# Building the experts' token lists in SBUF by one-hot matmuls, with slots of 128 tokens and another split of the early weights' subtraction

## The chip, the core and the metric

The kernel runs on one core of a Trainium2 chip, as one launch. The metric is the time of that launch on the device in microseconds (us). A core has a matrix engine (TensorE: PE for its matmuls, PEld for its weight loads in the profile), three elementwise engines (VectorE: DVE, ScalarE: ACT, GpSimd: POOL) and a queue engine (SyncE: SP) that here only issues transfers. Each engine works through its own instructions in order; semaphores hold one until another engine or a transfer is done.

## What is computed

A gated linear attention over 4 batches, 8 heads, 768 positions and head size 48, whose output rows (384 wide) go through a mixture of 8 experts with sticky routing:

```python
for t in range(S):                                   # attention
    state = alpha[:, :, t, :, None] * state + einsum('bhd,bhe->bhde', k[:, :, t], v[:, :, t])
    y[:, :, t] = einsum('bhd,bhde->bhe', q[:, :, t], state)
...
fresh_e = argmax(logits[b, s])                       # routing, token after token
e = fresh_e if s == 0 or local_gate[b, s] < 0.5 else prev_e
p = exp(ls) / (exp(ls).sum() + 1e-09)                # ls: logits less their largest
out[b, s] = p[e] * (relu(x[b, s] @ w1[e]) @ w2[e])   # w1: 384x1024, w2: 1024x384
```

So there are 3072 tokens, each for one expert, and which expert is known only after routing.

## The kernel before

**Attention.** 24 blocks of 128 tokens (`NB`), one after the other, four batches in turn (`G` = 4). The loop at L637 runs stages of several blocks in one turn: scans of alpha on DVE (`scan1`, `scan2`: tiles `A`, `sf`), their products with q and k on POOL (tile `x`), transposes and small matmuls on PE (`kt`, `pm`, `um`, `ym`, `xt`: PSUM tiles `kp`, `pe`, `up`, `y`, `xp`), masks and sums on DVE (`pq`, `st`), copies on ACT (`kk`, `sb`, `XR`, `vt`, `xx`). Each block's rows are stored to the DRAM tensor `xd`. From L629 to L695 instructions are pinned: every engine keeps the order in which the code was written.

**Side work.** `other()` (L589) is called three times a turn. It flushes deferred work (`later`), advances each running `route` by one piece (up to its next `yield`) and then either issues two filler matmuls (`dense`, on tile `dz`) or one piece of the early expert work.

**Routing.** `route(g)` (L417) handles a group of four blocks: logits (`lg`), transposes (`lt`, `rp`, `rb`), the sticky choice by a scan (`em`), one-hot of the expert (`oh`), softmax weight (`se`, `pn`, `pl`), prefix sums over tokens (`oi`, `pw`, `ps`, `po`) and, as `ix`, the row of each token in its expert's list. A list row holds the weight, the token's number and its row in `xd`. The lists live in the DRAM tensor `ls`, which is first filled with an empty entry (`fill`, L623 to L626); `route` scatters 128 entries for each block by an indirect DMA on POOL (L512).

**Experts.** A `Job` covers some rows of one expert's list in slots of 120 tokens: `load_list` reads rows of `ls` into `li` (SP), `gather` fetches the tokens' rows of `xd` (indirect DMA on POOL, tile `xg`), `trans` transposes them on PE (`tp`) and splits them into a high part (`xh`, ACT) and the rest (`xl`, DVE); `gemm1` makes `h` (72 matmuls, three for each product of split operands), split likewise into `hh` (ACT) and `hl` (DVE); `gemm2` makes `yp` (24 matmuls of 384 columns for a slot); `store` scales it by the weight (`yo`, DVE) and scatters it into `out` (indirect DMA on POOL). `Weights` loads an expert in seven pieces into staging tiles (`rw`, four buffers, on SP), takes the high part on ACT (`w1h`, `w2h`) and subtracts for the rest (`w1l`, `w2l`) on POOL or DVE.

**Early jobs.** `early()` (L526) starts once the first 12 blocks (`T1`) are routed. It runs three jobs within the attention's last part: the first 240 rows of expert 0 (job 0), the first 240 of expert 1 (job 1), and the other 240 of expert 1 (job 2), for which all blocks must be routed. Expert 1's subtractions run on POOL, as do those of expert 2 (`NEXT`). During the early jobs all transposes share one PSUM buffer (`tr`), with `kp` and `xp` of the attention. Behind them come experts 2 to 7 with 480 rows each and the other 240 rows of expert 0; there a scheduler sets the order.

**Tail.** A table of overflowing tokens is made (L721 to L732), and a loop that does not run with these data follows (L734).

Of the kernel before, what the change touches and what calls it, by code (L numbers as in the profile page):

```python
# [29 lines left out]
NS = CAP // SL  # L30
NOV = -(-(NTOK - CAP) // SL)
RS = CAP + NOV * SL
SENT = NTOK
ZTHR = -1.5 * 2.0 ** -23
# [5 lines left out]
C1 = 240  # L40
# [8 lines left out]
RW = 4  # L49
# [15 lines left out]
def gla_moe(ctx, tc, akq, vw, vn, wg, w1, w2, cst, tok, out):  # L65
# [28 lines left out]
    fill = cp.tile([SL, E * NS, 3], F32, name="fill")  # L94
# [15 lines left out]
    outs, lists, rest = [], [], []  # L110
# [47 lines left out]
    class Job:  # L158


        def __init__(self, e, r0, n, sp, ps, bx, bg, bh, by, pb, rows=NTOK + 1, bt=2, defer=lambda f: f()):
            self.e, self.r0, self.n, self.sp, self.ps = e, r0, n, sp, ps
            self.ns = n // SL
# [55 lines left out]
        def gemm2(self, W):  # L219
            for s in range(self.ns):  # L220
                w = slice(s * SL, (s + 1) * SL)
                yp = self.ps.tile([SL, DM], F32, tag=self.yt[s % len(self.yt)], bufs=self.pb[2], name=f"yp_{self.nm}_{s}")
# [8 lines left out]
                yo = self.sp.tile([SL, DM], F32, tag="yo", bufs=self.by, name=f"yo_{self.nm}_{s}")  # L231
# [10 lines left out]
    with ExitStack() as ac, ExitStack() as aa:  # L242
# [6 lines left out]
        dz = ap.tile([128, 512], F32R, bufs=1, name="dz")  # L249
# [3 lines left out]
        v_.tensor_copy(dz, z2[:, 0:512])  # L253
# [14 lines left out]
        st = {"c": c0}  # L268
        blk = {}
# [84 lines left out]
        def um(i):  # L354
# [3 lines left out]
            if i < G:  # L358
                s3 = ap.tile([R, 3, HP, D], F32, tag="st", bufs=G + 2, name=f"st_{i}")
# [57 lines left out]
        def route(g):  # L417
# [4 lines left out]
            def rt(shape, nm, dt=F32):  # L422
                return ap.tile(shape, dt, tag=nm, name=f"{nm}_{g}")
# [5 lines left out]
            lc = rt([128, 128], "lc")  # L429
# [14 lines left out]
            mb = mx.unsqueeze(2).broadcast_to([128, n, 8])  # L444
            ge = rt([128, n, 8], "ge")
            v_.tensor_tensor(ge, L8, mb, ALU.is_ge)
            v_.tensor_tensor(ge, ge, cc("desc").unsqueeze(1).broadcast_to([128, n, 8]), ALU.mult)
            m2 = rt([128, n], "m2")
            v_.tensor_reduce(m2, ge, AX.X, ALU.max)
            v_.tensor_tensor(ge, ge, m2.unsqueeze(2).broadcast_to([128, n, 8]), ALU.is_equal)  # L450
            zb = L[:, :, 8:9].broadcast_to([128, n, 8])
            v_.scalar_tensor_tensor(kr[:, 0], zb, ZTHR, ge, ALU.is_lt, ALU.mult)
            v_.tensor_single_scalar(kr[:, 1], zb, ZTHR, ALU.is_ge)
# [6 lines left out]
            km = rt([8 * n, 128], "km")  # L460
            s_.copy(km, rp[:, 1, :])
# [50 lines left out]
            for j in range(n):  # L512
# [3 lines left out]
                if j < n - 1:  # L516
                    yield
# [119 lines left out]
        for i in range(NB + 2):  # L637
# [4 lines left out]
            if i < NB:  # L642
                kt(i)
# [236 lines left out]
```

## Time and profile before

| | us |
|---|---|
| median of 3 runs | 498.49 (497.36 to 499.62) |
| the profiled execution | 495.6 |
| its span, first to last instruction | 493.8 |
| mean granted TensorE clock | 0.945 of full speed |

| engine | busy us | share of the span |
|---|---|---|
| PE | 434.4 | 88% |
| PEld | 391.0 | 79% |
| DVE | 250.2 | 51% |
| POOL | 232.2 | 47% |
| ACT | 181.1 | 37% |

A row of the profile's views reads: start and duration (or, for a group, busy time and mean ns), engine, source line, operation, the tile written `<-` the tiles read, sizes, count, and in brackets the idle time of the engine just before it with what ended that idle time. Most rows have one line, L79, since a wrapper records the operations: the tiles' names tell them apart.

### The profile page before, as it was taken

The numbers are of one execution on the slowest core, as the hardware profiler recorded it, in microseconds if no ns is written. First come the engines' busy times: TensorE is split into PE (matmuls) and PEld (weight loads), VectorE is DVE, ScalarE is ACT, GpSimd is POOL, SyncE is SP. The second block draws the span as 40 slices with busy tenths as digits, with TensorE's granted clock in tenths as the row PEclk, the third lists the DMA queues.
The fourth block names the chain that finished last, engine by engine and source line by source line (L and its number), as shares of the span: only waits on it lengthen the run. The fifth ranks groups of instructions, "written<-read, shape, count | busy, mean of one in ns | idle before, by whom it ended". The sixth has DMA issues, their size and how long they took to land.

```text
span 493.8 us, 10848 instructions
## 1 busy us (share of the span) xinstructions
PE 434.4 (88%) x4395; PEld 391.0 (79%) x4395; DVE 250.2 (51%) x440; ACT 181.1 (37%) x350; POOL 232.2 (47%) x245
## 2 busy tenths in 40 slices
PE   4999878989897888487979999999999999999990
PEld 4787767768775778486958998998998999989990
DVE  3878997989796526622222434334253253333320
ACT  1255654545443624221443423423334234233210
POOL 6453336464747335847385254353624735424201
PEclk9799998999988899798887999999999999999995
DMA  8789775797573011454155256254254452540100
GB/s 222 176 284 269 218 197 104 222 244 199 158 182 94 33 48 33 120 132 120 53 156 154 65 173 182 73 171 126 85 156 124 156 177 58 171 144 1 50 2 27
DMA packets 30058, 66.14 MB, mean 134 GB/s; under 512 B 7694, under 2 KB 13979, under 8 KB 30007
## 3 DMA queue, kind: packets, MB, share of 16 engines
q1 hardware_dynamic: 20022, 49.70, 36.7%
q0 software_dynamic: 4864, 10.66, 7.4%
q10 hardware_dynamic: 5121, 5.07, 3.1%
q8 instruction: 35, 0.57, 0.5%
q14 instruction: 16, 0.13, 0.1%
HBM read 55.89 MB, written 10.70 MB: 135 GB/s over the span
## 4 chain that ended last, share of the span: by engine, by line
PE 52%; issue 10%; DVE 7%; POOL 2%; ACT 2%; DMA 1%; POOLq 0%; ACTq 0%; DVEq 0%
PE h L79 23%; PE yp L79 21%; PE y L79 3%; PE tp L79 2%; DMA ls<-pl,ix 1%; PE up L79 1%; POOL out L79 1%; DVE sf L79 1%; DVE A L79 1%; PE pe L79 1%; PE lg L79 1%; DVE hl L79 1%; POOL w1l_0b L79 1%; DVE xl L79 1%; DVE oi L79 1%
## 5 line engine op out<-in xcount | busy, mean ns | idle before, releaser
L79 DVE SCALAR_TENSOR_TENSOR hl<-h,hh 128x480 fp32r<-128x480 f32 (+1 forms) x80 | 44.2, 555 | 91.5 <-ACT hh L79 82.7
L79 ACT ACTIVATE hh<-h 128x480 fp32r<-128x480 f32 (+1 forms) x80 | 39.0, 490 | 89.8 <-PE h L79 79.9
L79 POOL DMA_INDIRECT xg<-xd,li x32 | 34.8, 1088 | 48.9 <-DMA li<-ls 25.2
L79 POOL DMA_INDIRECT out<-yo,li x32 | 32.5, 1016 | 47.7 <-DVE yo L79 42.9
L79 DVE TENSOR_SCALAR yo<-yp,li 120x384 f32<-120x384 f32 x32 | 19.6, 617 | 63.9 <-PE yp L79 61.6
L79 POOL TENSOR_TENSOR x<-x,sf 112x512 f32<-112x512 f32 x24 | 28.9, 1205 | 32.8 <-DVE sf L79 32.8
L79 POOL TENSOR_TENSOR x<-x,A 112x512 f32<-112x512 f32 x24 | 29.3, 1221 | 29.2 <-DVE A L79 8.7
L79 DVE TENSOR_TENSOR_SCAN A<-a,z 112x520 f32<-112x520 f32 x24 | 32.5, 1352 | 6.8 <-POOL a L79 6.8
L79 PE MATMUL h<-dz 128*128 128x240 f32 x142 | 33.0, 337 | 2.3 <-DVE z L79 2.3
L79 POOL DMA_INDIRECT ls<-pl,ix x24 | 25.5, 1061 | 18.6 <-DVE hl L79 7.8
L79 DVE TENSOR_TENSOR_SCAN sf<-a,z 112x520 f32<-112x520 f32 x24 | 33.8, 1407 | 0.1
L79 PE MATMUL y<-vt,pq 64*64 64x48 f32 x768 | 30.0, 224 | 3.3 <-issue 3.3
L79 PEld LDWEIGHTS y<-vt,pq 64*64 64x64 f32 x768 | 26.1, 138 | 8.2 <-issue 8.0
L79 ACT COPY sb<-st 48x384 f32<-48x384 f32 x48 | 24.5, 510 | 15.3 <-DVE st L79 14.7
L79 PE MATMUL y<-sb,x 112*64 112x96 f32 x384 | 23.8, 270 | 6.2 <-ACT sb L79 6.1
L79 PEld LDWEIGHTS h<-dz 128*128 128x128 f32 x142 | 22.5, 213 | 6.9 <-DVE z L79 2.3
L79 PE MATMUL tp<-cs,xg 120*128 120x120 f32 x96 | 14.8, 282 | 12.3 <-DVE xl L79 12.3
L79 PEld LDWEIGHTS y<-sb,x 112*64 112x64 f32 x384 | 18.7, 149 | 8.5 <-ACT sb L79 7.2
L79 PE MATMUL up<-vt,kk 128*48 128x96 f32 (+1 forms) x384 | 23.3, 269 | 0.0
L79 PEld LDWEIGHTS tp<-cs,xg 120*128 120x128 f32 x96 | 11.5, 146 | 14.9 <-DVE xl L79 13.8
L79 DVE TENSOR_TENSOR xl<-tp,xh 128x360 fp32r<-128x360 f32 x32 | 16.0, 526 | 11.6 <-ACT xh L79 10.2
L79 ACT COPY XR<-y 128x384 f32<-128x384 f32 x24 | 11.5, 480 | 27.7 <-PE y L79 22.0
(229 smaller groups left out, 1235.0 us busy)
## 6 DMA issues: line engine op xcount, KB each, us to landing
x<-akq SPq DMA_DIRECT2D x24, 448.0 KB
a<-akq SPq DMA_DIRECT2D x24, 227.9 KB
vt<-vn SPq DMA_DIRECT2D x24, 192.0 KB
xd<-XR ACTq DMA_DIRECT2D x24, 192.0 KB
rw_0a<-w SPq DMA_DIRECT2D x3, 512.0 KB
rw_0a<-w SPq DMA_DIRECT2D x4, 384.0 KB
rw_1a<-w SPq DMA_DIRECT2D x3, 512.0 KB
rw_1a<-w SPq DMA_DIRECT2D x4, 384.0 KB
```

Source lines behind the costliest of these rows:

```text
L79: r = f(*a, **k)
```

## The change

- **Lists in SBUF.** `route` no longer scatters. From the token's place (`plc`) it works out the list's slot column (`sl`) and the row in the slot (`rr`), builds one-hots of both (`oa`: 32 columns, `on`: 128 rows), multiplies the slot one-hot with the token's three values (`vo`), and four matmuls (`lp`: on transposed times vo, 96 columns) add the entries at their places; `acc` sums them over the groups, and `idx` holds the token numbers and rows as whole numbers. For the first five groups `on` is made on ACT (two activations for a block) and `vo` on POOL, for the last both on DVE. The filling of `ls` and the read of it (`load_list`'s DMA) are gone; `load_list` now only names slices of `idx` and `acc`. The scatter of all lists stands in the overflow branch, which does not run.
- **Slots of 128.** `TS` = 128: a job of 480 rows has slots of 128, 128, 128 and 96; jobs 0 and 1 have 256 rows, job 2 and the last job 224. `dz` and the filler matmuls are 256 wide.
- **Early weights.** Expert 1's and expert 2's subtractions run on DVE, and there are three staging buffers instead of four (`RW`).
- **Order.** `route` is a piece shorter up to `rb`; deferred work is flushed earlier in the turn; `early` starts with fewer empty pieces; transposes of the next job are put between matmuls of `gemm2`, not behind each other; constants are set up in the first blocks (`made`).

```diff
-RW = 4
+RW = 3
+TS = 128
+NS = -(-CAP // TS)
+WH = 1.5 * 2.0 ** 23
-C1 = 240
+C1 = 256
...
-        def load_list(self):
-            self.li = self.sp.tile([SL, self.ns, 3], F32, tag="li", bufs=self.bx, name=f"li_{self.nm}")
-            r = self.e * RS + self.r0
-            y_.dma_start(self.li, ls[r:r + self.n].rearrange("(p s) c -> p s c", p=SL))
+        def load_list(self, v):
+            c = slice(self.r0 // TS, self.r0 // TS + self.ns)
+            self.tok, self.row = (idx[:, v, k, self.e, c] for k in range(2))
+            self.pr = acc[:, 0, self.e, c]
...
+            pl = vals[:, g * n:(g + 1) * n]
-            g_.tensor_copy(pl.bitcast(I32)[:, :, 1], tk[:, 2 * g:2 * NB:2 * NBB])
-            g_.tensor_copy(pl.bitcast(I32)[:, :, 2], tk[:, 2 * g * G + 1:2 * (g + 1) * G:2])
...
-            for j in range(n):
-                apart(lists, g_.indirect_dma_start(
-                    out=ls[:, :], out_offset=bass.IndirectOffsetOnAxis(ap=ix[:, j:j + 1], axis=0),
-                    in_=pl[:, j, :], in_offset=None, bounds_check=E * RS - 1, oob_is_err=False))
+            pt = rt([128, n], "pt")
+            v_.tensor_scalar(pt, pc, 1.0 / TS, None, ALU.mult)
+            sl = rt([128, n], "sl")
+            v_.tensor_scalar(sl, pt, -(TS - 1) / (2.0 * TS), WH, ALU.add, ALU.add)
+            rr = rt([128, n], "rr")
+            v_.scalar_tensor_tensor(rr, sl, WH, pt, ALU.subtract, ALU.subtract)
+            oa = rt([128, n, E * NS], "oa", bufs=1)
+            v_.tensor_tensor(oa, ioa.rearrange("p e s -> p (e s)").unsqueeze(1).broadcast_to([128, n, E * NS]),
+                             sl.unsqueeze(2).broadcast_to([128, n, E * NS]), ALU.is_equal)
+            yield
+            (v_ if end else g_).tensor_tensor(vo, oa.unsqueeze(2).broadcast_to([128, n, 3, E * NS]),
+                                              pl.unsqueeze(3).broadcast_to([128, n, 3, E * NS]), ALU.mult)
+            if end:
+                v_.tensor_tensor(on, iob.unsqueeze(1).broadcast_to([128, n, TS]),
+                                 rr.unsqueeze(2).broadcast_to([128, n, TS]), ALU.is_equal)
+            else:
+                for j in range(n):
+                    s_.activation(on[:, j], iob, AF.Abs, bias=rr[:, j:j + 1], scale=-1.0)
+                    s_.activation(on[:, j], on[:, j], AF.Relu, bias=one[:, 0:1], scale=-float(TS))
+                    if j < n - 1:
+                        yield
+            yield
+            for j in range(n):
+                t_.matmul(lp, lhsT=on[:, j], rhs=vo[:, j].rearrange("p k s -> p (k s)"), start=(j == 0), stop=(j == n - 1))
+            v_.tensor_tensor(af, af, lp, ALU.add)
+            if end or (g + 1) * G == T1:
+                v_.tensor_tensor(idx[:, int(end)], acc[:, 1:3], off, ALU.add)
...
                     if k % 4 < 2 or k == 2:
                         next(ws, None)
+                    if next(ts, True) is None:
+                        yield False
+                    if not nx and k == 1:
+                        ts = rest[0].trans()
...
+                    if nx and k == (6 if nx.r0 else 3):
+                        ts = nx.trans()
...
-                    begin(NEXT, g_)
+                    begin(NEXT, v_)
...
-                begin(EARLY[1], g_)
+                begin(EARLY[1], v_)
```

Where instructions stand now. The first place is DVE between job 0's last `hl` and job 1's first. Before, from the group's choice to the first transposed slot of job 1:

```order
L79 SCALAR_TENSOR_TENSOR em_2989<-km_2973,em_2699,rp_2970 32x128
L79 TENSOR_TENSOR ex_2925<-L_2902,mx_2926 128x32
L79 SCALAR_TENSOR_TENSOR oi_3025<-m_73,oh_105 128x40
L79 TENSOR_REDUCE se_3028<-ex_2925 128x4
L79 TENSOR_SCALAR se_3028<-se_3028 128x4
L79 RECIPROCAL se_3028<-se_3028 128x4
L79 TENSOR_SCALAR yo_0_0_3045<-yp_0_0_2992,li_0_2345 120x384
...
L79 TENSOR_REDUCE ix_3077<-po_3080 128x4
L79 TENSOR_TENSOR xl_0_3087<-tp_0_0_3088,xh_0_3086 128x3x120
L79 TENSOR_TENSOR xl_0_3087<-tp_0_1_3098,xh_0_3086 128x3x120
```

In the changed kernel, on DVE, the same stretch up to that slot:

```order
L81 TENSOR_TENSOR w1l_1a_3035<-rw_1a_1557,w1h_1a_3034 128x1024
L81 TENSOR_TENSOR acc<-acc,lp_3044 128x96
L81 TENSOR_TENSOR w1l_1a_3053<-rw_1a_1559,w1h_1a_3052 128x1024
L81 TENSOR_TENSOR w1l_1a_3071<-rw_1a_1561,w1h_1a_3070 128x1024
L81 TENSOR_SCALAR yo_0_0_3079<-yp_0_0_3013,acc 128x384
L81 SCALAR_TENSOR_TENSOR em_3085<-km_3065,em_2770,rp_3062 32x128
L81 TENSOR_TENSOR w2l_1a_3100<-rw_1a_3050,w2h_1a_3099 128x768
L81 TENSOR_TENSOR xl_0_3103<-tp_0_0_3104,xh_0_3102 128x3x128
L81 SCALAR_TENSOR_TENSOR oi_3111<-m_80,oh_112 128x40
```

The subtractions of expert 1 (`w1l_1a`, `w2l_1a`) now stand on DVE ahead of `em`, and the transposed slot's rest stands ahead of `oi`. Further on DVE, behind the list's last place, the changed kernel has these rows, for which there was none before but the `yo`:

```order
L81 TENSOR_REDUCE plc<-po_3150 128x4
L81 TENSOR_SCALAR pt_3153<-plc 128x4
L81 TENSOR_SCALAR sl_3155<-pt_3153 128x4
L81 SCALAR_TENSOR_TENSOR rr_3157<-sl_3155,pt_3153 128x4
L81 TENSOR_TENSOR oa_3159<-ioa,sl_3155 128x128
L81 TENSOR_SCALAR yo_0_1_3167<-yp_0_1_3087,acc 128x384
L81 TENSOR_TENSOR vo_3172<-oa_3159,vals 128x384
L81 TENSOR_TENSOR on_3174<-iob,rr_3157 128x512
L81 TENSOR_TENSOR w2l_1a_3177<-rw_1a_3097,w2h_1a_3176 128x768
L81 TENSOR_TENSOR acc<-acc,lp_3180 128x96
```

They end in the last group's lists. On PE, job 1's two transposes before, within job 0's second slot:

```order
L79 MATMUL yp_0_1_3055<-w2h_0a_1177,hl_0_3_2894 120x384
L79 MATMUL tp_0_0_3088<-cs,xg_0_0_2904 128x120 x3
L79 MATMUL tp_0_1_3098<-cs,xg_0_1_2936 128x120 x3
L79 MATMUL yp_0_1_3055<-w2h_0a_1315,hh_0_4_2917 120x384
```

and in the changed kernel, on PE, around the same two:

```order
L81 MATMUL rb_3094<-cs,em_3085 128x32
L81 MATMUL tp_0_0_3104<-cs,xg_0_0_2905 128x128 x3
...
L81 MATMUL yp_0_1_3087<-w2l_0a_1202,hh_0_3_2865 128x384
L81 MATMUL yp_0_1_3087<-w2h_0a_1201,hl_0_3_2866 128x384
L81 MATMUL tp_0_1_3132<-cs,xg_0_1_2935 128x128 x3
L81 MATMUL pw_3139<-oi_3111,one 128x40
```

Six matmuls now stand between the two transposes, and `rb` and `pw` of the last group stand next to them.

More of the change, by code (lines that the diff above doesn't have):

```diff
@@ L93, in gla_moe @@
     wgs = cp.tile([128, 3, 32], F32, name="wgs")
[L94 removed]
+    fill = cp.tile([SL, 3], F32, name="fill")
+    vals = cp.tile([128, NB, 3], F32, name="vals")
+    plc = cp.tile([128, NB], F32, name="plc")
+    acc = cp.tile([128, 3, E, NS], F32, name="acc")
+    off = cp.tile([128, 2, E, NS], F32, name="off")
+    idx = cp.tile([128, 2, 2, E, NS], I32, name="idx")
+    ioa = cp.tile([128, E, NS], F32, name="ioa")
+    iob = cp.tile([128, TS], F32, name="iob")
     cntp = cp.tile([8, 1], F32, name="cntp")
@@ L108, in gla_moe @@
     ident = cc("ident")
-    outs, lists, rest = [], [], []
+    outs, rest = [], []
     def apart(those, w):
@@ L162, in __init__ @@
             self.e, self.r0, self.n, self.sp, self.ps = e, r0, n, sp, ps
-            self.ns = n // SL
+            self.ns = -(-n // TS)
+            self.w = [slice(s * TS, min(n, (s + 1) * TS)) for s in range(self.ns)]
+            self.m = [w.stop - w.start for w in self.w]
             self.bx, self.bg, self.bh, self.by, self.pb = bx, bg, bh, by, pb
@@ L268, in gla_moe @@
         st = {"c": c0}
+        sts = [ap.tile([R, 3, HP, D], F32, tag="st", bufs=G + 1, name=f"st_{i}") for i in range(G)]
         blk = {}
@@ L504, in route @@
             v_.tensor_tensor(po, ps[:, :, 0:n].rearrange("p e b -> p b e"), ob, ALU.mult)
-            with nc.allow_low_precision(reason="whole numbers, one of them not zero"):
-                v_.tensor_reduce(ix, po, AX.X, ALU.add)
+            pc = plc[:, g * n:(g + 1) * n]
+            v_.tensor_reduce(pc, po, AX.X, ALU.add)
             st["c"] = ps[:, :, n]
@@ L521, in begin @@
         def begin(e, sub):
-            EW[e] = Weights(e, f"{e}a", 4, later.append, sub)
-            for _ in range(4):
+            EW[e] = Weights(e, f"{e}a", RW, later.append, sub)
+            for _ in range(RW):
                 EW[e].load()
@@ L550, in early @@
                     yield True
+                    if not nx and k == 2:
+                        rest[0].load_list(1)
+                    if not nx and k == 5:
+                        for _ in rest[0].gather():
+                            pass
                     if nx and nx.r0 == 0 and k == 2:
@@ L650, in gla_moe @@
                 drained[0] = True
+            for _ in range(min(3, len(made))):
+                made.pop(0)()
             other(i >= NB)
@@ L757, in gla_moe @@
         v_.tensor_copy(ei[:, NOV:], tab[0:1, 0, :])
+        px = mp.tile([128, NB], I32, bufs=1, name="px")
+        v_.tensor_copy(px, plc)
+        pv = mp.tile([128, NB, 3], F32, bufs=1, name="pv")
+        v_.tensor_copy(pv[:, :, 0], vals[:, :, 0])
+        v_.tensor_scalar(pv.bitcast(I32)[:, :, 1], vals[:, :, 1], float(SENT), None, ALU.add)
+        v_.tensor_copy(pv.bitcast(I32)[:, :, 2], vals[:, :, 2])
+        lists = []
+        for i in range(NB):
+            apart(lists, g_.indirect_dma_start(
+                out=ls[:, :], out_offset=bass.IndirectOffsetOnAxis(ap=px[:, i:i + 1], axis=0),
+                in_=pv[:, i, :], in_offset=None, bounds_check=E * RS - 1, oob_is_err=False))
         with tc.For_i(0, NT, 1) as i:
```

129 lines of the change are left out of this document (64 added, 65 removed).

## The prediction

> **What bounds the kernel now.** I read the busy time by stage first, cut where the program's stages begin on PE. The columns are a stretch and its length, then the busy time of each engine with its instructions, PE's granted clock, and the DMA engines' share and rate.
>
> ```profile
> core 0: us, PE busy (x) PEld busy (x) DVE busy (x) ACT busy (x) POOL busy (x), PEclk, DMA share, GB/s
> 19.93:69.18 49.25, 44.70 (x905) 37.46 (x904) 42.55 (x67) 26.85 (x56) 20.81 (x30) 1.00 0.82 238
> 69.18:98.69 29.51, 25.76 (x469) 21.23 (x468) 25.48 (x50) 14.69 (x32) 14.89 (x20) 0.94 0.62 161
> 98.69:124.94 26.25, 23.59 (x469) 19.62 (x468) 24.12 (x45) 12.69 (x30) 14.87 (x18) 1.00 0.84 231
> 124.94:152.01 27.07, 22.35 (x452) 18.54 (x451) 22.86 (x45) 12.18 (x30) 16.41 (x20) 0.94 0.63 162
> 152.01:176.10 24.09, 20.15 (x357) 16.61 (x356) 12.40 (x31) 11.14 (x26) 10.78 (x11) 0.86 0.17 51
> 176.10:207.53 31.43, 22.66 (x165) 21.11 (x166) 16.79 (x33) 11.37 (x24) 17.16 (x14) 0.89 0.23 66
> 207.53:227.31 19.78, 17.33 (x124) 16.82 (x124) 4.53 (x13) 2.98 (x8) 11.74 (x9) 1.00 0.43 110
> 227.31:243.73 16.42, 12.57 (x78) 11.46 (x77) 4.39 (x10) 3.41 (x9) 8.52 (x8) 0.79 0.34 97
> 243.73:260.08 16.35, 11.91 (x62) 10.55 (x61) 3.82 (x8) 8.73 (x13) 11.69 (x6) 0.84 0.47 128
> 260.08:281.13 21.05, 21.05 (x95) 18.40 (x96) 7.91 (x13) 8.11 (x16) 7.10 (x5) 0.88 0.43 120
> 281.13:480.80 199.67, 199.67 (x1104) 188.03 (x1102) 73.83 (x116) 65.72 (x105) 84.40 (x59) 1.00 0.39 114
> ```
>
> From 281.13 to 480.80 PE is never idle at full clock, and its matmuls there are the same in number and in moving columns after the change, so nothing is to be had in those 199.67 us. In the attention (to 152.01) DVE is busy for 84 to 92% and PE for 83 to 91%: both fill. From 152.01 to 260.08 neither does; PE is idle 3.9, 8.8, 2.5, 3.9 and 4.4 us in the five stretches, and its clock falls. The gain has to come from these and from DVE's waits in the attention.
>
> Next, the timeline (start, duration, engine, operation, and the idle time before it with its cause) and the groups of POOL and PE.
>
> ```profile
> L79 POOL DMA_INDIRECT ls<-pl,ix x24 | 25.5, 1061 | 18.6 <-DVE hl L79 7.8
> L79 PE MATMUL tp<-cs,xg 120*128 120x120 f32 x96 | 14.8, 282 | 12.3 <-DVE xl L79 12.3
> 80.27 0.69 DVE L79 TENSOR_TENSOR pq<-pe,cs 128x512 f32<-128x512 f32 x1 [2.61 <-remote]
> 134.34 0.69 DVE L79 TENSOR_TENSOR pq<-pe,cs 128x512 f32<-128x512 f32 x1 [2.68 <-remote]
> 159.89 0.36 DVE L79 TENSOR_TENSOR st<-up,st 112x192 f32<-112x192 f32 x1 [3.85 <-remote]
> 192.36 4.76 POOL L79 TENSOR_TENSOR w1l_1a<-rw_1a,w1h_1a 128x1024 fp32r<-128x1024 f32 x2 [5.71 <-ACT oh L79]
> 192.39 2.48 DVE L79 TENSOR_TENSOR_SCAN oi<-m,oh 128x40 f32<-128x40 f32 x1 [1.31 <-ACT oh L79]
> 200.09 0.19 DVE L79 TENSOR_TENSOR ps<-pw,ps 128x40 f32<-128x40 f32 x1
> 203.54 0.86 PE L79 MATMUL tp<-cs,xg 120*128 120x120 f32 x3 [6.34 <-DVE xl L79]
> ```
>
> The 24 scatters come in six bursts of four, and the "remote" waits stand where a burst is going on: 2.61 and 2.68 us in the first and third, 3.85 in the fourth. Beside a subtraction on POOL (2.38 us each) the small scan `oi` takes 2.48 us, where the small `ps` without one takes 0.19. The last group's choice, prefix sums and `xl` all stand in that row of DVE, and PE waits 6.34 us for the `xl`.
>
> **The change part by part**, against the profiled 495.6 us (2.9 below the median of 498.49).
>
> *Start, -1.0.* The filling of `ls` goes out of POOL's way.
>
> ```profile
> 7.41 0.23 POOL L79 COPY fill<-tk 120x32 int32<-120x32 int32 x1 [1.10 <-DMA tk<-tok]
> ```
>
> POOL waits 1.10 us for `tk` there, with the memset behind it that DVE's first `A` needs. Ends: 0 (the start is bound by a transfer) and -1.3 (wait and copy).
>
> *First eight blocks, +0.4.* Some fourteen constants are set up beside 42.55 of 49.25 us of DVE work, three of them on DVE; with `ps` for each that is 0.6, and 0.2 of it I take as hidden. The ends are 0 and, by `pq` (0.69), 2.1.
>
> *Middle of the attention, -3.7.* In each group the four scatters go, and DVE gets four small operations and `acc` more than it loses: 5 x 0.19 = 1.0 by `ps`, at most 5 x 0.69 = 3.5 by `pq`. I take the smaller, since `pt`, `sl` and `rr` are 128x4. DVE's waits go: 2.61 + 2.68 and, in the second burst, some 1.4 less 0.
>
> ```profile
> DVE pq L79 <- PE pe L79: 1.4, 1, 1.4
> ```
>
> That row (waits of DVE from 98.69 to 124.94: total, times, longest) is all that DVE waits there. So 29.51 becomes 27.9, 26.25 becomes 25.9 and 27.07 becomes 25.4: -3.7 in all. Ends: -6.7 (what is added lies in what is left of DVE's idle time) and +1 (the chain of the blocks keeps its pace, and what is added is paid for). The eight activations that make `on` cost ACT 8 x 0.26 by the row below, in stretches in which it is idle for half the time; POOL gets `vo` (128x384, below the 1.22 us of `x`) for four scatters of 1.06. Either only delays `lp`, and nothing waits for `lp` until a job reads its list.
>
> ```profile
> L79 ACT COPY lc<-lg 128x128 f32<-128x128 f32 x6 | 1.5, 258 | 1.2 <-PE lg L79 1.2
> L79 POOL TENSOR_TENSOR x<-x,A 112x512 f32<-112x512 f32 x24 | 29.3, 1221 | 29.2 <-DVE A L79 8.7
> ```
>
> *Last four blocks, +1.5.* Without the read of `ls` and with fewer empty pieces job 0 starts earlier: 36 of its 72 matmuls for `h` now stand ahead of the last `y`. The chain of work gives their time:
>
> ```profile
> 260.08 8.31 PE h L79 x27
> 329.86 5.90 PE h L79 x27
> ```
>
> 5.90 / 27 x 256/480 x 36 = 4.2 us, and 0.4 for `lp`, against 3.9 us of idle PE. If every gap could be filled the stretch would grow by 0.7; I take 1.5. Ends: 0 and 4.6.
>
> *The seam, 31.43 to 27.0, -4.4.* PE's 22.66 us lose those 4.2: 18.5. Four waits stand in DVE's new order:
>
> ```profile
> L79 DVE TENSOR_TENSOR w1l_0a<-rw_0a,w1h_0a 128x1024 fp32r<-128x1024 f32 x3 | 4.8, 1592 | 2.1 <-ACT w1h_0a L79 2.1
> L79 DVE TENSOR_TENSOR w2l_7b<-rw_7b,w2h_7b 128x768 fp32r<-128x768 f32 x4 | 3.8, 959 | 3.8 <-ACT w2h_7b L79 3.7
> ```
>
> Expert 1's rest now costs DVE 3 x 1.59 + 4 x 0.96 = 8.6 us in the seam, where POOL did it before, and the small operations no longer take 2 us each. Queued behind it: `em`, for which PE's `rb` waits, some 1.6 (one `w1l`); `xl` behind a `w2l`, 1.3 with the copy; `pw` for `oi`, 0.6; `lp` for `on` and the last `w2l`, 3.0 (the 128x512 `on` about as `pq`, two products, and a `w2l`). 18.5 + 6.5 = 25.0, and I add 2.0 for waits too small to be told apart, as DVE has nearly 20 us of work there. Ends: 23 (half of the waits lie under PE's queue) and 31.4 (DVE's row as long as the old one).
>
> *Job 1, -2.3; job 2, -3.0; expert 2's transposes, -2.0; its first matmuls, -1.0.* Transposes now stand between matmuls of `gemm2`, so that `xl` is made beside them. What PE waited for, and its clock in two pieces of these stretches:
>
> ```profile
> 215.61 0.38 PE L79 MATMUL h<-xh,w1h_1a 128*128 128x240 f32 x1 [1.59 <-DVE hl L79]
> 228.79 0.53 PE L79 MATMUL tp<-cs,xg 120*128 120x120 f32 x3 [1.17 <-DVE xl L79]
> 252.94 0.53 PE L79 MATMUL tp<-cs,xg 120*128 120x120 f32 x3 [1.41 <-DVE xl L79]
> 203.50:207.50 4.00, 3.96 (x15) 3.94 (x16) 0.53 (x1) 1.92 (x3) 2.95 (x3) 0.57 0.43 132
> 233.00:237.50 4.50, 4.40 (x20) 4.41 (x21) 0.45 (x2) 0.37 (x1) 3.56 (x4) 0.50 0.48 134
> ```
>
> Job 1 loses its idle 2.45, less what `hl` still costs. Job 2 has 3.9 of idle time and 2.2 lost to a clock of 0.50 for 4.4 us; half goes. Expert 2's 4.4 of idle time would go too, but its 8.6 us of subtraction now stand on DVE with four `xl` and the `yo`, nearly as long as `gemm2`: I take 2.0. Its first `h` group took 8.31 where a later one takes 5.90; 1.0 of the 2.4 goes. Ends together: -15 (all idle time and all slow clock) and -1.
>
> The trace has 4.4 us at half clock from 233.00 on, though no wait ahead of it is above 1.2 us. The Trainium skill (TensorE: Matmul & The Clock Gate, "HAM oscillation — how this bites in real kernels") warns only of idle gaps above about 3.4 us. The 6.34 us gap followed by 0.57 agrees with it, 233.00 does not; I go by the trace.
>
> Sum: -1.0 + 0.4 - 3.7 + 1.5 - 4.4 - 2.3 - 3.0 - 2.0 - 1.0 = -15.5: 480.1 in the profiled execution, and **483.0** beside the median of 498.49.
>
> **The rivals.** *The clock stays full* (470, between 466 and 475). The seam's waits are single and short now, and the 8 us lost to slow clock (1.7, 2.2, 2.4 and what lies between) all go, with the middle's last 3 us. For it: the only long wait, 6.34, goes. Against it: 233.00. By the skill's rule above, this would be the outcome.
>
> *DVE takes the waits' place* (488 to 496, about 492). DVE carries 17.2 us more in the seam and behind it, and 1 us in each group. If each small operation waits for a 1.59 us subtraction, seam, job 2 and expert 2 keep their length: 483.0 + 4.4 + 3.0 + 2.0 = 492.4. For it: the DVE of the middle is 84 to 92% busy. Against it: from 176.10 to 260.08 it is busy for 29.5 of 84 us.
>
> *The scatters were hidden anyway, no change* (496 to 501). Every stretch is bound by the blocks' chain, and the early jobs wait for the weights. The stretch without a burst (19.93 to 69.18) has 6.2 us a block, those with one 7.4, 6.6 and 6.8, which speaks against it.
>
> *Slower: three staging buffers.* A layer's seven pieces come every 199.67 / 6 / 7 = 4.75 us, and a cast waits for its transfer:
>
> ```profile
> 387.55 1.05 ACT L79 CAST w1h_7b<-rw_7b 128x1024 fp32r<-128x1024 f32 x1 [3.71 <-DMA rw_7b<-w]
> 399.48 0.84 ACT L79 CAST w2h_7b<-rw_7b 128x768 fp32r<-128x768 f32 x1 [3.42 <-DMA rw_7b<-w]
> ```
>
> PE does not wait for it now. With one buffer less each load is issued a piece later; if that uncovers one wait of 3.71 us in each of six layers, 22 us are added to PE's unbroken stretch: 483.0 + 22 = 505. It decides from where a transfer comes more than some 3 us (two thirds of a piece's period) later than now. Against it: the DMA share there is 0.39.
>
> **How the numbers follow.** The forecast (475 to 488) has 0.55: most of its terms have a wait in a row that goes. The full clock has 0.17, DVE in the waits' place 0.18, no change 0.04, slower 0.06. About 0.5% (2.5 us) is what a measurement of this kernel can tell from no change, so faster is 0.55 + 0.17 + 0.18 = 0.90, same 0.04, slower 0.06. The range of 469 to 493 takes in the forecast and most of its two neighbours (0.12 and 0.13 of them), and leaves out the tail of both and what is not faster.
>
> **What would show it.** No "remote" wait of DVE from 69 to 160, and blocks 8 to 19 in 79 instead of 82.8 us; half of job 0's `h` ahead of the last `y`; no wait of PE above 3 us in the seam and the seam below 28; `tp` without waits for `xl`; PE without a gap in the six layers. It is wrong if DVE's waits in the middle come back under other names, if `em`, `xl` or `hl` stand behind subtractions for longer than one of them, or if `w1h` of the later experts delays PE.

## The result, and the profile after

The changed kernel took 482.17 us (median of 4 runs, 481.29 to 484.0) beside 497.93 for the kernel before (494.44 to 499.62): a ratio of 0.9735, with an interval from 0.9687 to 0.9782. 483.0 had been forecast, in a range of 469 to 493. The profiled execution was the slowest of the four, 484.0 us with a span of 482.2, 11.6 less than the span before.

The windows view of the changed kernel, cut at the same places of the program as the rows of before (length, then busy time of each engine, PE's clock, DMA):

```profile
core 0: us, PE busy (x) PEld busy (x) DVE busy (x) ACT busy (x) POOL busy (x), PEclk, DMA share, GB/s
...
18.54:69.33 50.79, 46.37 (x906) 38.88 (x905) 42.87 (x72) 27.13 (x56) 22.13 (x35) 0.97 0.75 217
69.33:96.72 27.39, 24.48 (x477) 20.49 (x476) 24.78 (x53) 17.78 (x41) 12.71 (x12) 1.00 0.67 192
96.72:121.81 25.09, 24.36 (x477) 20.51 (x477) 22.96 (x55) 15.47 (x39) 12.72 (x15) 1.00 0.78 235
121.81:144.23 22.42, 21.60 (x459) 17.96 (x459) 21.52 (x40) 14.46 (x36) 12.56 (x13) 1.00 0.67 193
144.23:175.65 31.42, 25.84 (x401) 21.77 (x400) 14.72 (x41) 15.18 (x38) 9.40 (x8) 0.89 0.14 39
175.65:201.30 25.65, 19.29 (x146) 17.17 (x146) 16.24 (x46) 12.82 (x28) 2.92 (x3) 1.00 0.34 100
201.30:223.25 21.95, 20.30 (x123) 19.59 (x123) 5.76 (x15) 3.07 (x8) 11.01 (x11) 0.84 0.50 144
223.25:239.19 15.94, 12.49 (x79) 11.41 (x78) 4.34 (x10) 3.38 (x9) 0.99 (x1) 0.79 0.02 6
239.19:251.24 12.05, 10.47 (x62) 8.87 (x61) 8.98 (x14) 7.43 (x11) 5.20 (x5) 1.00 0.59 186
251.24:269.46 18.22, 18.22 (x91) 16.00 (x92) 7.36 (x11) 7.53 (x14) 7.81 (x6) 1.00 0.63 191
269.46:469.30 199.84, 199.84 (x1104) 186.11 (x1103) 75.84 (x120) 66.56 (x108) 74.84 (x51) 1.00 0.37 110
```

| stage | before, us | forecast change | after, us | change |
|---|---|---|---|---|
| start | 19.93 | -1.0 | 18.54 | -1.4 |
| first eight blocks | 49.25 | +0.4 | 50.79 | +1.5 |
| middle, y8 to y20 | 82.83 | -3.7 | 74.90 | -7.9 |
| last four blocks | 24.09 | +1.5 | 31.42 | +7.3 |
| seam | 31.43 | -4.4 | 25.65 | -5.8 |
| job 1 | 19.78 | -2.3 | 21.95 | +2.2 |
| job 2 | 16.42 | -3.0 | 15.94 | -0.5 |
| expert 2's transposes | 16.35 | -2.0 | 12.05 | -4.3 |
| its first matmuls | 21.05 | -1.0 | 18.22 | -2.8 |
| six layers | 199.67 | 0 | 199.84 | +0.2 |

The sum hides larger moves: the last blocks give nearly all of the middle's gain back, and what is left is gained in the seam and around expert 2. Rows of the timeline of the changed kernel, from the last blocks through the seam to job 2:

```profile
169.84 0.38 PE L81 MATMUL h<-xh,w1h_0a 128*128 128x256 f32 x1 [0.78 <-DVE hl L81]
192.16 0.22 PE L81 MATMUL rb<-cs,em 32*128 32x32 f32 x1 [1.58 <-DVE em L81]
194.70 0.23 DVE L81 TENSOR_TENSOR_SCAN oi<-m,oh 128x40 f32<-128x40 f32 x1
194.84 0.55 PE L81 MATMUL tp<-cs,xg 128*128 128x128 f32 x3 [0.93 <-DVE xl L81]
195.04 0.17 DVE L81 TENSOR_SCALAR se<-se 128x4 f32<-128x4 f32 x1
200.42 1.10 PE L81 MATMUL lp<-vo,on 128*128 128x96 f32 x8 [2.50 <-DVE on L81]
224.96 0.47 PE L81 MATMUL tp<-cs,xg 96*128 96x96 f32 x3 [1.22 <-DVE xl L81]
```

`oi` takes 0.23 us instead of 2.48, and the one gap of 6.34 us has become three of 1.58, 0.93 and 2.50 us. The transposes as a group wait far less for `xl` (12.3 us before):

```profile
L81 PE MATMUL tp<-cs,xg 128*128 128x128 f32 (+1 forms) x96 | 14.6, 274 | 2.9 <-DVE xl L81 2.7
```

### The profile page after: what moved, and what is told of

It reads as the page before. It is cut to its first block, busy times and chain, and to the rows that moved or that the text cites. A ratio compares the mean times of both kernels' runs of the same rounds, so it can differ in the third digit from the quotient of the medians.

```text
span 482.2 us, 10873 instructions
## 1 busy us (share of the span) xinstructions
PE 437.9 (91%) x4443; PEld 391.5 (81%) x4443; DVE 257.3 (53%) x485; ACT 194.1 (40%) x390; POOL 186.7 (39%) x207
## 4 chain that ended last, share of the span: by engine, by line
PE 53%; issue 11%; DVE 9%; ACT 3%; POOL 2%; POOLq 0%; DVEq 0%; ACTq 0%
PE h L81 24%; PE yp L81 20%; PE y L81 3%; PE tp L81 2%; DVE A L81 2%; POOL out L81 1%; PE up L81 1%; DVE st L81 1%; DVE sf L81 1%; DVE pq L81 1%; ACT hh L81 1%; POOL w1l_0b L81 1%; PE pe L81 1%; DVE xl L81 1%; PE lp L81 1%
## 5 line engine op out<-in xcount | busy, mean ns | idle before, releaser
L81 DVE SCALAR_TENSOR_TENSOR hl<-h,hh 128x480 fp32r<-128x480 f32 (+2 forms) x80 | 43.9, 556 | 77.2 <-ACT hh L81 76.9
L81 ACT ACTIVATE hh<-h 128x480 fp32r<-128x480 f32 (+2 forms) x80 | 38.7, 490 | 82.4 <-PE h L81 82.3
L81 POOL DMA_INDIRECT out<-yo,idx x32 | 32.5, 1017 | 80.5 <-DVE yo L81 78.0
L81 POOL DMA_INDIRECT xg<-xd,idx x32 | 32.6, 1018 | 61.0 <-PE tp L81 52.9
L81 DVE TENSOR_SCALAR yo<-yp,acc 128x384 f32<-128x384 f32 (+1 forms) x32 | 19.6, 616 | 61.1 <-PE yp L81 61.0
L81 PE MATMUL h<-dz 128*128 128x256 f32 x142 | 35.0, 354 | 2.1 <-DVE z L81 2.1
L81 PEld LDWEIGHTS up<-vt,kk 128*48 128x48 f32 (+1 forms) x384 | 18.3, 140 | 3.4 <-issue 1.0
L81 ACT COPY kk<-kp 128x448 f32<-128x448 f32 x24 | 12.8, 531 | 20.7 <-PE kp L81 20.6
L81 PE MATMUL h<-xh,w1h_1a 128*128 128x256 f32 (+1 forms) x48 | 16.4, 342 | 3.9 <-DVE hl L81 2.7
L81 ACT CAST xh<-tp 128x384 fp32r<-128x384 f32 (+1 forms) x32 | 14.0, 462 | 13.9 <-PE tp L81 13.6
```

The source lines that it names most:

```text
L81: r = f(*a, **k)
```

## The experiments

Twelve kernels ran, in four sets; each set had its own runs of the kernel before, whose median went from 495.7 to 502.5 us, so ratios to it are compared and not times; the brackets hold 95% intervals. Unedited, the changed kernel came to 0.9735 and, in another set, to 0.9694.

**The changed kernel again.**

> The changed kernel itself, unedited, as the mark for the other runs of this call: 480 to 484 us. It also shows which parts of its profile belong to one execution only: by the theory that the half clock follows lulls of PE, the phases behind the waits for on (near 202) and for job 2's xl (near 225) come again, while others may move.

485.33 us, 0.9694 (0.9572 to 0.9816). The stages agree within 0.4 us but for job 1 (26.7 us instead of 24.6 up to job 2's first matmul), where PE had a gap of 3.04 us that the other profile has not; ACT, which makes `hh` there, waits 2.80 us for what the profile calls "remote", in a kernel without any scatter into lists. Both profiles have half clock at 58.5 to 62.5, 154 to 161.5 and 202 to 209 us; the fourth phase moved from 225.5 to 229, along with job 2's first wait.

**Subtractions back on POOL.** Edit of the changed kernel:

```diff
-                    begin(NEXT, v_)
+                    begin(NEXT, g_)
...
-                begin(EARLY[1], v_)
+                begin(EARLY[1], g_)
```

> The changed kernel with the subtractions of experts 1 and 2 back on POOL; all else as changed. Theory (a small DVE operation beside a POOL subtraction is held for as long as that runs, and the seam's chain em, oi, ps, on is made of them): the seam, 25.65 us in the changed kernel, becomes 29 to 32 us, with oi or se above 1.5 us instead of 0.2, the stretch of expert 2's transposes (12.05) becomes 13 to 15, and the whole 4 to 9 us slower than the changed kernel (486 to 491). Rival (it is the scatters' absence alone that frees the small operations): within 1.5 us of 482. Second rival (the subtractions stand in DVE's way): 2 to 4 us faster, as PE's waits for em (1.58) and on (2.50) go.

486.85 us, 0.9824 (0.9766 to 0.9882), by the ratios 4 to 6 us above the two results of the changed kernel, though the intervals overlap. In its timeline:

```profile
188.77 0.46 DVE L81 TENSOR_TENSOR_SCAN em<-km,em,rp 32x128 f32<-32x128 f32 x1
193.43 4.27 DVE L81 TENSOR_SCALAR se<-se 128x4 f32<-128x4 f32 x1
194.03 3.62 POOL L81 TENSOR_TENSOR w2l_1a<-rw_1a,w2h_1a 128x768 fp32r<-128x768 f32 x2
202.01 1.99 PE L81 MATMUL lp<-vo,on 128*128 128x96 f32 x8 [4.11 <-DVE on L81]
```

The seam in its windows:

```profile
174.70:203.71 29.01, 21.54 (x147) 19.64 (x146) 14.31 (x40) 13.01 (x28) 15.17 (x9) 0.88 0.31 90
```

The first theory holds for the seam in the main: 29.01 us instead of 25.65, with a 128x4 operation of 4.27 us, and behind it PE waits 4.11 us for `on` instead of 2.50. Not all of the loss is that hold. PE also waits 2.17 us for `xl` instead of 0.93 (there `xh` stands on ACT behind a cast that waited for its transfer), and the seam ran at half clock from 193.5 to 197 and from 200.5 on, where the changed kernel has full clock. Expert 2's transposes hardly lose (12.49 instead of 12.05). `rb` came without a wait, as the second rival had it, but the rest cost more.

**The same edit from the other side**, in the kernel before (`g_` to `v_` in both calls of `begin`).

> The kernel before with one edit: the subtractions of experts 1 and 2 on DVE. Theory (the same as for the return to POOL, from the other side): the seam 31.43 becomes 27 to 29, the oi and se rows fall from 2 us to 0.2, the gap of 6.34 us of PE becomes below 3.5, and the whole 3 to 6 us faster than before (0.988 to 0.994). Rival (the chain is as long, since em and oi stand behind subtractions of 1.2 to 1.6 us each in DVE's row instead): within 1.5 us of the kernel before.

498.26 us, 1.0048 (1.0003 to 1.0093): no gain. Its seam did become 26.9 us, but job 1 lost what the seam had won. In its timeline:

```profile
210.69 0.17 DVE L79 TENSOR_TENSOR gt<-cntp,cs 8x22 f32<-8x22 f32 x1 [5.71 <-DMA rw_2a<-w]
211.42 0.52 PE L79 MATMUL h<-xh,w1h_1a 128*128 128x240 f32 x1 [3.15 <-DVE hl L79]
```

In its windows, job 1 and then the three groups of blocks:

```profile
202.05:227.87 25.82, 20.13 (x122) 19.34 (x122) 6.24 (x15) 2.98 (x9) 13.97 (x13) 0.87 0.44 115
69.45:96.44 26.99, 23.19 (x469) 19.38 (x468) 26.31 (x50) 14.57 (x32) 15.60 (x17) 1.00 0.71 179
96.44:122.09 25.65, 23.13 (x469) 19.39 (x469) 22.49 (x45) 12.38 (x29) 15.22 (x20) 1.00 0.96 248
122.09:152.49 30.40, 26.96 (x452) 22.78 (x451) 23.46 (x48) 13.61 (x31) 19.00 (x21) 0.74 0.53 145
```

Neither theory had this. `gt` is an operation of the tail that stands early in DVE's row; its tile takes over memory of the attention's pool, so it waits for all who used that pool, and `hl` stands behind it. (The row names a load of weights as what ended the wait; the run with the scatters' sources out of the way, below, tells the two apart.) And two groups of blocks with all their scatters took 26.99 and 25.65 us, with no "remote" wait. The third took 30.40: in POOL's row the product `x` stood behind the burst of scatters, and PE waited for it:

```profile
134.75 0.60 PE L79 MATMUL kp<-cs,x 112*128 112x112 f32 x4 [3.14 <-POOL x L79]
```

A phase of half clock of some 20 us begins at 136.5, right behind that wait.

**Scatters put back into the changed kernel**: four for each group, beside the new lists.

```diff
+            ix = rt([128, n], "ix", I32)
+            v_.tensor_copy(ix, pc)
...
+                apart(early_lists, g_.indirect_dma_start(
+                    out=ls[:, :], out_offset=bass.IndirectOffsetOnAxis(ap=ix[:, j:j + 1], axis=0),
+                    in_=pl[:, j, :], in_offset=None, bounds_check=E * RS - 1, oob_is_err=False))
```

> The changed kernel with the 24 scatters into the lists in DRAM put back beside the new lists (one small conversion on DVE and four scatters on POOL in each group), so that only their cost is added. Theory (the scatters held up the blocks): the three groups of blocks from y8 to y20, 74.90 us in the changed kernel, become 79 to 83 (82.83 before), with 'remote' waits of DVE of 2 us and more, and the whole 5 to 10 us slower than the changed kernel. Rival (the blocks became faster by the shorter route, the smaller POOL load or the order, and the scatters were hidden): 75 to 76 us there, and the whole within 1.5 us of 482.

520.58 us, 1.0488 (1.0416 to 1.0561): worse than any theory. y8 to y20 took 96.5 us, and there was no "remote" wait at all. DVE's and PE's waits in this kernel (in total, times, longest):

```profile
DVE sf L81 <- POOL x L81: 14.1, 4, 4.1
...
PE kp L81 <- POOL x L81: 9.5, 3, 3.5
```

POOL makes `x`; with `vo` and the scatters in its row, `x` is late, and `sf` waits for its buffer. So this run does not price the scatters of the kernel before: it shows only that both jobs don't fit into POOL's row.

**The kernel before without its scatters** (the call of `indirect_dma_start` on `ls` left out).

> The kernel before without its 24 scatters; the lists stay empty, so the experts work on the filling row and nothing is written to the output, and only the time up to the end of job 1 can be read against the kernel before. Theory (the scatters on POOL hold up the blocks, as the remote waits of 2.6 us suggest): y8 to y20 takes 75 to 79 us instead of 82.83. Rival, suggested by the kernel before with only its subtractions moved, whose y8 to y16 took 52.6 us with all its scatters there (52.5 in the changed kernel, 55.8 in the profile of before): the scatters are hidden in the middle and the remote waits belong to one execution; then 52 to 53 for y8 to y16. For the end of the attention: DVE's gt, which waits until the last scatter has landed before it may use its memory, no longer holds up hl; job 1 has no wait above 1 us.

492.3 us, 0.9789 (0.9668 to 0.991), of which only the part to the end of job 1 says anything, and job 1's first matmul came at 206.84 us (207.53 with scatters). Its three groups of blocks and its seam:

```profile
69.24:96.43 27.19, 24.60 (x470) 20.54 (x469) 25.34 (x50) 14.37 (x32) 10.63 (x16) 0.94 0.62 178
96.43:126.18 29.75, 27.43 (x469) 23.08 (x468) 21.90 (x47) 13.39 (x31) 10.21 (x15) 0.83 0.70 203
126.18:149.91 23.73, 20.58 (x451) 17.42 (x450) 21.98 (x43) 12.20 (x30) 12.61 (x16) 0.96 0.61 181
171.69:206.84 35.15, 25.72 (x166) 24.18 (x166) 18.53 (x33) 11.36 (x24) 11.91 (x8) 0.80 0.24 70
```

y8 to y16 took 56.9 us, more than with scatters after the subtractions had moved (52.6); 14.5 us of it ran at half clock, so this run does not decide between theory and rival. In job 1 `gt` no longer waited (it took 3.64 us beside POOL's subtractions), and PE's longest wait for `hl` was 1.01 us instead of 1.59. The seam was no shorter either: its long wait for `xl` (8.11 us here) is put down to the subtractions, which stayed on POOL here; this run alone does not show it.

**Transposes together again** in the changed kernel: `ts = ...trans()` replaced by the loops of before (job 1's at `k == 5`, job 2's at `k == 7`, expert 2's at `k == 6`).

> The changed kernel with the next job's transposes behind each other again, where they stood before, instead of between matmuls of gemm2. Theory (with one buffer for tp PE waits 1.1 to 1.4 us for each xl, and the interleaving hides that): four to five such waits come back in the seam and from 239 to 251, 3 to 6 us slower than the changed kernel (485 to 488), half of it in the stretch of expert 2's transposes. Rival (those stretches are set by the subtractions and by the casts, and the waits only move): within 1.5 us of 482.

489.25 us, 0.9873 (0.9815 to 0.993), some 7 us above the changed kernel. From job 2's `gemm2` to expert 2's `gemm1`, first in its windows:

```profile
236.67:254.35 17.68, 11.92 (x63) 10.07 (x61) 9.16 (x14) 9.01 (x13) 6.04 (x5) 0.81 0.54 163
```

and the transposes of that stretch in its timeline:

```profile
247.11 0.55 PE L81 MATMUL tp<-cs,xg 128*128 128x128 f32 x3 [2.64 <-DVE xl L81]
248.82 0.90 PE L81 MATMUL tp<-cs,xg 128*128 128x128 f32 x3 [1.16 <-DVE xl L81]
250.89 0.74 PE L81 MATMUL tp<-cs,xg 96*128 96x96 f32 x3 [1.16 <-DVE xl L81]
```

17.68 instead of 12.05, and half clock from 247.5 to 258. The theory was right, its price somewhat low: the clock came on top of the waits.

**Both order edits in the kernel before**, lists still in DRAM: subtractions on DVE, and the changed kernel's loop over `gemm2` with its `ts`.

> The kernel before with two parts of the change and without the third: subtractions of experts 1 and 2 on DVE, and the next job's transposes between matmuls of gemm2; the lists stay in DRAM with their scatters, the slots stay at 120. Theory (most of the gain comes from the transposes: putting them together again cost the changed kernel 7 us): 5 to 8 us faster than the kernel before (0.984 to 0.990), with 12 to 13 us from job 2's gemm2 to expert 2's gemm1 instead of 16.35, and that expert's first matmuls at full clock; the lists account for the rest, 0.010 to 0.015. Rival (the gain is the lists' and the transposes only matter with them): within 2 us of the kernel before, as with the subtractions alone.

498.1 us, 1.0043 (1.0 to 1.0085): the rival's number. Its profile has a span of 504.2 us and long phases of half clock (one from 59.5 to 80), so only single waits and stages at full clock are read from it. In its timeline, job 1:

```profile
228.22 0.57 PE L79 MATMUL h<-xh,w1h_1a 128*128 128x240 f32 x1 [5.71 <-DVE hl L79]
```

and in its windows, job 2's `gemm2` with expert 2's transposes:

```profile
260.74:272.69 11.95, 10.46 (x62) 9.14 (x61) 9.03 (x14) 7.98 (x12) 1.00 (x1) 1.00 0.46 142
```

Expert 2's transposes had their gain (11.95 instead of 16.35); job 1 lost it, in one wait for the `hl` behind `gt`.

**The same, with the scatters' sources out of the way.**

```diff
-            pl = rt([128, n, 3], "pl")
+            pl = cp.tile([128, n, 3], F32, tag="pl", bufs=2, name=f"pl_{g}")
...
-            ix = rt([128, n], "ix", I32)
+            ix = cp.tile([128, n], I32, tag="ix", bufs=2, name=f"ix_{g}")
```

> The run before's kernel (lists in DRAM with their scatters, slots of 120, subtractions on DVE, transposes between matmuls) with one edit: the scatters' sources pl and ix lie in memory that is kept to the end, so that DVE's gt, whose memory is taken over from the attention's, no longer waits for the last scatters to land. Theory (the scatters cost their time there, in job 1, and hardly in the blocks): the wait of PE for hl (5.71 us in the run before, 3.15 with the subtractions alone) goes, job 1's first matmuls take 12 to 14 us instead of 17.4 and 20.9, and the whole is 6 to 11 us faster than the kernel before (0.978 to 0.988), half or more of what the whole change gives, with the lists still in DRAM. Rival (gt waits for the transfers of expert 2's weights, as the view of waits names it, or job 1 waits for the lists themselves): no change against the run before, 1.00.

484.81 us, 0.9661 (0.9597 to 0.9724): with all lists in DRAM, all 24 scatters, slots of 120 and four buffers, the whole gain of the change, and more than the theory's 0.978 to 0.988. In its timeline:

```profile
80.63 0.69 DVE L79 TENSOR_TENSOR pq<-pe,cs 128x512 f32<-128x512 f32 x1 [2.51 <-remote]
...
206.75 0.17 DVE L79 TENSOR_TENSOR gt<-cntp,cs 8x22 f32<-8x22 f32 x1
```

In its windows, job 1, its matmuls up to `gemm2`, and the first of the three groups:

```profile
203.73:223.40 19.67, 17.13 (x123) 16.62 (x122) 6.43 (x15) 2.91 (x9) 8.41 (x8) 1.00 0.47 114
203.73:215.00 11.27, 8.73 (x75) 8.26 (x75) 5.35 (x13) 2.54 (x8) 4.08 (x4) 1.00 0.62 149
69.64:99.86 30.22, 27.07 (x469) 22.29 (x468) 24.96 (x50) 14.78 (x32) 14.85 (x20) 0.89 0.59 153
```

`gt` no longer waits (the last scatter was issued at 206.58), so the wait was for the scatters' sources and not for the weights. Job 1 takes 19.67 us, where it took 25.82 with the subtractions alone and, in its profile of long half clock, 29.28 with both order edits. That is up to 10 of the 19 us by which the ratios put this run below the one before; the rest is not accounted for. The "remote" waits are here again, three of them.

**The seam's lulls filled** in the changed kernel with unused matmuls: `dense(10)` ahead of the last group's `rb`, `dense(18)` ahead of its `lp`.

> The changed kernel with unused matmuls (10 ahead of the last group's rb, 18 ahead of its lp, into the tile of the filler) in the two longest waits of the seam. Theory (half clock follows lulls of PE, here 1.58 and 2.49 us): the phase of half clock from 202 to 209 goes and job 1 takes 18.5 to 20 us instead of 21.95, the whole 1.5 to 3 us faster than the changed kernel. Rival (the clock falls for reasons other than PE's lulls, or the filler delays what it stands ahead of): within 1 us, or up to 1 us slower.

486.83 us, 0.9739 (0.9659 to 0.9819): no faster. The half clock did go from job 1's first part (first row here; 13.62 us in the changed kernel), but its profile has 14 us of it in the first eight blocks, which the edit does not touch, and 10.5 us from 157.5 on.

```profile
206.11:217.62 11.51, 9.32 (x75) 8.84 (x75) 3.85 (x11) 1.92 (x5) 7.82 (x8) 1.00 0.68 199
```

**Job 2's transposes earlier** in the changed kernel: its list and gather in job 1's `gemm1`, and

```diff
-                    if nx and k == (6 if nx.r0 else 3):
+                    if nx and k == (2 if nx.r0 else 3):
                         ts = nx.trans()
```

> The changed kernel with job 2's list read and gathered during job 1's first matmuls and its transposes put between matmuls of job 1's gemm2, as the change did for the others. Theory: the waits of 1.22 and 0.48 us for its xl and xh go, and with that lull the half clock behind it (225.5 to 233): 2 to 5 us faster than the changed kernel. Rival (the waits go and the clock falls all the same, at the waits of 0.87 for hl): 1.5 to 2 us faster. Second rival (the gathers, now earlier, delay expert 2's weights or the stores): no gain.

479.16 us, 0.962 (0.9481 to 0.9758), 6 us below the changed kernel of the same set (four runs of each, 476.3 to 483.2 beside 481.4 to 487.3). From job 1's `gemm2` to job 2's, in two windows:

```profile
211.72:221.06 9.34, 9.19 (x56) 8.83 (x55) 2.81 (x6) 1.92 (x5) 1.02 (x1) 1.00 0.13 44
221.06:231.35 10.29, 8.54 (x73) 8.18 (x73) 3.32 (x8) 2.50 (x7) 0.99 (x1) 1.00 0.03 9
```

19.63 us where the changed kernel takes 24.27, all at full clock.

**With expert 1's `w2l` after the seam** (its steps moved into job 1's `gemm1`, and `begin(NEXT, v_)` behind them).

> The changed kernel with job 2's transposes between matmuls of job 1's gemm2 (as in the run before, there some 6 us faster) and with the four subtractions for expert 1's w2 moved from the seam into job 1's first matmuls. Theory (the chain of the last group's list, oi to on, stands behind those subtractions on DVE): PE's wait for on falls from 2.5 to below 1.3 us, the seam from 25.65 to 23.5 to 24.5, the whole 1 to 2 us below the run with the transposes alone (474 to 479). Rival (the subtractions then delay hl in job 1, or the loads for expert 2 come too late): what the seam wins, job 1 or expert 2's first matmuls lose.

477.63 us, 0.9617 (0.9507 to 0.9727), not told apart from the run before. PE's wait for `on` fell as the theory had it, and the seam took 24.19 us:

```profile
201.05 1.10 PE L81 MATMUL lp<-vo,on 128*128 128x96 f32 x8 [0.80 <-DVE on L81]
```

From the last `y` to job 1's `gemm2` it took 33.84 us, where the run with early transposes alone took 39.99; but part of that difference is a phase of half clock from 198 to 205 in the other profile, which is missing here. And PE waited 1.66 us for `hl` and 2.00 for `xl` in job 1: part of the win is lost there, as the rival said.

**With fill in three lulls** as well (10 ahead of block 22's `kp`, 10 ahead of `rb`, 6 ahead of `lp`).

> The same with unused matmuls in three lulls: 10 ahead of kp of block 22, 10 ahead of the last group's rb, 6 ahead of its lp. Theory (the half clock follows lulls of PE above a microsecond): no phase of half clock from 150 to 215, y20 to the last y 28 us or below, job 1 to its gemm2 in 11.5 instead of 13.6 to 15.7 us, the whole 1.5 to 4 us below the run without the fill. Rival (the phases come at their own times): the same total within 1.5 us, with phases elsewhere.

475.79 us, 0.9628 (0.9509 to 0.9747). The profile has no half clock from 17 to 214 us, and 4 us of it behind. y20 to the last `y` took 28.32 us (31.42 in the changed kernel), as in the run with early transposes alone (28.09), so the total does not tell the fill from no fill. These three versions have the lowest ratios of the study, with intervals that overlap that of the run with the lists kept.

## Why the prediction came out right

The median was forecast within 1 us, but that is in part luck: stage by stage the profiles differ by 11.6 us and not by the 15.5 of the sum, since the execution profiled before was 2.9 us faster than its median and the one after 1.8 slower. And the 3.9 us between the sums is what is left of errors of both signs that add up to some 24 us. Of the signs named beforehand one failed: the transposes still wait for `xl`, 2.7 us in three waits.

- **Start (-1.0; -1.4) and first eight blocks (+0.4; +1.5).** The first was right. In the blocks, both profiles of the changed kernel have half clock from 58.5 to 62.5, and the one of before has none there.
- **Seam (-4.4; -5.8): right, by the mechanism named.** The waits were put at 1.6, 1.3, 0.6 and 3.0 us and measured 1.58, 0.93, none and 2.50. A subtraction took 1.22 us with POOL quiet, not 1.59. One item was wrong: the `w2l` that I put into the wait for `on` stands behind `on` in DVE's row; two others, earlier in the list's chain, are what it waits for, and with them moved away the wait was 0.80. The return to POOL shows the cause in part (4.11 instead of 2.50, beside another wait and the clock).
- **Expert 2's transposes and first matmuls (-3.0 together; -7.1): right mechanism, sized too low.** I kept half of the idle time for the subtractions on DVE; they fitted beside the matmuls, and the first matmuls ran at full clock (0.88 before). Putting the transposes together again brought it all back in their stretch: 17.68 us, where the kernel before took 16.35.
- **Job 2 (-3.0; -0.5): wrong step.** "Transposes now stand between matmuls of `gemm2`" does not hold for job 2: its first stands behind the last of them, and PE waited 1.22 us for `xl` and ran at half clock behind it. The edit that makes the sentence true brought 4.6 us.
- **Job 1 (-2.3; +2.2): wrong, in the clock and in the waits.** The half clock from 202 to 209 follows the wait of 2.50 us; with the lull filled, the first part took 11.51 instead of 13.62. But 11.51 is no better than the 11.21 of before: PE's idle time, which was to go, fell only from 2.45 to 1.65 (waits of 0.72 us for `cntp` and 0.93 for `hl` stayed).
- **Last four blocks (+1.5; +7.3): beyond the bound of 4.6.** I let 36 matmuls fill the gaps. But groups of nine wait for `hl` in PE's row (0.78 and 0.93 us, and 0.93 once more just behind the last `y`) with the blocks' work behind them, PE waited 1.86 us ahead of one `kp`, and a phase of half clock from 154 to 161.5 lies there; without that phase the early-transposes kernel took 28.09, still 4.0 more than before.
- **Middle (-3.7; -7.9): the sign was right, the place only in part.** The table gives the three groups, and in brackets how much of each ran at half clock. With half of the bracket taken off (an estimate), the sums are 78.8 for before, 77.5 with the lists kept, 74.8 with the subtractions moved, 72.4 without scatters and 74.9 for the change.

| kernel | y8 to y12 | y12 to y16 | y16 to y20 | "remote" waits of DVE |
|---|---|---|---|---|
| before | 29.51 (4) | 26.25 | 27.07 (4) | 2 |
| lists kept | 30.22 (7.5) | 25.73 | 27.28 (4) | 3 |
| subtractions moved, all scatters | 26.99 | 25.65 | 30.40 (16.5) | 0 |
| no scatters | 27.19 (4) | 29.75 (10.5) | 23.73 (2) | 0 |
| changed | 27.39 | 25.09 | 22.42 | 0 |

So the "remote" waits beside scatters are not in every profile. Where they are, the three groups together take some 3 to 4 us more by that estimate than in the changed kernel, and in four of five cases a phase of half clock follows. Without them, the first two groups with all scatters are as fast as the changed ones; the third is not, as PE there waits 3.14 us for the `x` behind the burst, and the estimate, which takes 8 us off it, is generous to it. What the scatters cost in the blocks stays open between these profiles, one of each kernel.

- **Layers and tail (0): right.** ACT now waits up to 8.2 us for the transfer of an expert's `w1`, where the same cast waited 4.7 before (3.7 to 7.1 for the row that the prediction shows). The waits grew by some 3.5 us, more than the 3 us from which the rival of three buffers feared a gap of PE, and PE's stretch is still without one, so the rival fell.

```profile
ACT w1h_4b L81 <- DMA rw_4b<-w: 8.2, 1, 8.2
```

What I did not see at all is, by the ratios, the largest effect of the lists' move. The chain of waits of the kernel before has it, and DVE's row in its timeline:

```profile
207.70 6.18 DMA ls<-pl,ix
214.35 0.17 DVE L79 TENSOR_TENSOR gt<-cntp,cs 8x22 f32<-8x22 f32 x1 [2.55 <-POOL w2l_1a L79]
```

From the last scatter on, DVE's `gt` waits for the landing, with `hl` behind it and PE's next matmuls behind that. PE lost 1.59 us there in the kernel before; with the subtractions moved, and so an earlier job 1, it lost 3.15 and 5.71 us, and half clock followed. So the order edits alone gave nothing, twice. With the wait taken away, by lists in SBUF or by two tiles in other memory, they pay. In the changed kernel `gt` runs at 203.98 without a wait. What stays open is what the slots of 128 are worth alone, which wasn't tried, and what the profile calls "remote"; it is not tied to the lists' scatters, as ACT's 2.80 us in the second profile of the changed kernel show.

## What to carry to other kernels

An edit that pays nothing alone may be waiting for another: look behind each wait that you take away for what was hidden under it, above all for small operations that take over memory from a transfer still under way and stand in the middle of an engine's row. A gain can be sized only together with the clock: each lull of PE of 1.5 to 2.5 us that is left may cost as much again behind it (here 2.50 us, and then 2.1 in job 1's first part), though filling two of them did not make the whole faster. Before lists or tables are rebuilt elsewhere, try whether moving the buffers that the transfers read is enough.

## What the runs showed of the hardware

**Phases of half clock follow some short lulls of PE, in steps.** Read off windows of 0.5 us, the phases at 0.50 after the start are 3.5 to 4, 7 to 7.5, 10.5, 14 or more than 20 us long, and PE is often fully busy in them. In the changed kernel (both profiles) the gap of 1.86 us at 150.45 is followed by 154 to 161.5, and the gap of 2.50 at 197.93 by 202 to 209; with the second filled, the phase there is gone, and with both filled, both. Not every such gap has one: the kernel with early transposes has the same gap of 1.86 us and no phase behind it. The Trainium skill (TensorE: Matmul & The Clock Gate, "What's actually happening") has windows of about 3.4 us, which agrees with the steps; it has the clock fall after an idle window, and here gaps of 1.2 to 2.5 us were enough. The changed kernel's profile has 26 us of such phases and that of before 40, so at most some 7 of the 11.6 us between the two are the clock's (an estimate: half of the difference).

**Which DVE operations POOL holds.** Beside POOL's subtractions, `em` (0.46 us, reads PSUM) ran unhindered, while the scaling of `se` (128x4, in SBUF alone) took 4.27 instead of 0.17: it ended at 197.70, when POOL's second subtraction ended (197.65). The Trainium skill (SBUF — State Buffer, "SBUF: two separate sides") has one port pair that VectorE and GpSimd lock for a whole instruction; these rows agree with it.

**Prices that differed.** An `on` activation took 0.40 us, not the 0.26 of a copy of that size, and `vo` on POOL 1.58 in the mean (0.83 the shortest, 1.76 the longest), not below 1.22; no wait of PE names either.
